# Second layer of a fused attention + MLP kernel: 128x128 matmuls among the scores, or 64x64 products with a written order for VectorE and ScalarE

## The chip, the cores and the metric

One core of one Trainium2 chip. The metric is the device time of one execution in microseconds (us), the median of the runs shown; lower is better.

## The reference

Attention with a root-mean-square norm of q and k over the head dimension, then a two-layer MLP with the tanh form of gelu. Eight batches, 12 heads, 448 positions, head dimension 64; `d_model` 768, `d_ff` 2048.

```python
q_n, k_n = rmsnorm(q, g_q), rmsnorm(k, g_k)            # x / sqrt(mean(x*x) + 1e-6) * g
scores = matmul(q_n, k_n.T) / sqrt(64)
attn = exp(scores - max(scores)); attn = attn / (sum(attn) + 1e-9)
x = matmul(attn, v).transpose(0, 2, 1, 3).reshape(8 * 448, 768)
h = x @ w_in                                            # 768 -> 2048
g = 0.5 * h * (1 + tanh(sqrt(2 / pi) * (h + 0.044715 * h**3)))
out = g @ w_out                                         # 2048 -> 768, float32
```

## The kernel before

The weights stay in SBUF in bf16 (`win`, `wout`). Batches go one after the other. Of each batch the 12 heads are three groups of four (index `c`), and the 448 keys are seven slices of 64 (index `t`): a *unit* (c, t) is four 64x64 matmuls of 448 columns, side by side in the array (two heads by two rows of the array), which give the scores of four heads for 64 keys, keys on the partitions. ScalarE turns a unit into exps (`ex`, L337; a constant `shift` takes the place of the maximum). VectorE adds the exps of a group over its slices (`key_sums`, L353 to L359), so that the sum over keys is one 64x64 step with a matrix of ones in place of seven; `products` (L384) makes the sums (`what` 0) or the values (`what` 1, seven steps of four matmuls). `turned`, `recip` and `spread` (L393, L399, L404) make the reciprocal of the sums and spread it over the partitions with VectorE's transposes; `quad_x` (L417) multiplies the values by it, into `xT`.

The first layer: 16 slices `f` of `d_ff`, six matmuls of 128x128 by 448 columns each. `mm1_pair` (L482) makes two slices in a PSUM tile of two banks with one gelu of 896 (L487); `mm1` (L431) one slice with one gelu of 448 (L437). From batch 2 on slices 0 to 3 go in pairs, 4 to 15 singly. The results go to `g`, which holds two batches, 896 rows, that is seven tiles of 128 rows.

The second layer (`mm2`, L452) takes a tile `i` of 128 rows and half of the 768 columns: 16 matmuls of 128x128 by 384 columns, summed over `f` in a bank of `ps_m`, copied to `osb` by VectorE (L462) or ScalarE (L460) and stored by SyncE. It lags: the second layer of a batch is laid among the scores of the next batch's attention.

The order is written by hand (`manual_schedule`): what Python records is what each engine's queue holds. `attention` (L511) lays out eight groups of units (`cuts`), and after each a number of second-layer matmuls (`shares`, `upto`): 96 in all in attention 2 (b = 1), 112 in each of attentions 3 to 8. So TensorE alternates between units or products, in the 64x64 form, and `mm2`, in the 128x128 form. `side` and `behind` hold what else is recorded at a group: loads two or three batches ahead, norms of the next batch, totals of squares. PSUM has eight banks: three tiles of two banks (`rounds`, taken in turn by `pair`) and two banks of `ps_m` in the steady part. GpSimd makes norms (L273), squares (L161) and the loads of v; `gpsimd_waits` makes it wait for a given tile by copying one element of it (`mark`, L673).

The first attention (`first_attention`) has another order and is not touched but for `unit` being cut in two, and for the place of one load of v. After the last first layer, 144 matmuls of the second layer remain; they end the kernel.

Of the kernel before, what the change touches and what calls it, by code (L numbers as in the profile page):

```python
# [17 lines left out]
def kernel(  # L18
# [19 lines left out]
    P = 128  # L38
# [23 lines left out]
    ps_m = ctx.enter_context(tc.tile_pool(name="ps_m", bufs=2, space=bass.MemoryType.PSUM))  # L62
    ps_t = ctx.enter_context(tc.tile_pool(name="ps_t", bufs=1, space=bass.MemoryType.PSUM))
    start = ctx.enter_context(ExitStack())
    ps_o = start.enter_context(tc.tile_pool(name="ps_o", bufs=1, space=bass.MemoryType.PSUM))
# [8 lines left out]
    def three():  # L74
        return len(rounds) == 3
# [164 lines left out]
    def rsqrt_last(b):  # L240
# [4 lines left out]
        if three():  # L245
            own, dst = pair("root")[:, 0], y
        else:
            own, dst = oall[0][:, S:], place(b, 1)
# [73 lines left out]
    exs, ess, oas = {}, {}, {}  # L322

    def unit(b, c, t):

        if (b, c) not in exs:
            exs[b, c] = exq.tile([P, NT, 2, S], BF16, tag="ex", name="ex")
        ex = exs[b, c]
        sc = pair("sc")
        for a in range(2):  # L330
            rs = slice(a * D, (a + 1) * D)
            for r in range(2):
                nc.tensor.matmul(  # L333
                    sc[r * R:(r + 1) * R, a, :S], kT[rs, c, t, r], qT[b][rs, c, :, r],
                    start=True, stop=True,
                )
        nc.scalar.activation(ex[:, t], sc[:, :, :S], AF.Exp, scale=scale, bias=shift)  # L337

    def added(b, c):

        return NT - 1 if b > 1 else (NT - 1, 0, NT - 2)[c] if b else 0

    def key_sums(b, c, t):

        n = added(b, c)
        if t > n or t == 0:
            return
        ex = exs[b, c]
        if t == 1:
            ess[b, c] = exq.tile([P, 2, S], BF16, tag="es", name="es")  # L350
        es = ess[b, c]
        if t == 1:
            nc.vector.tensor_add(es, ex[:, 0], ex[:, 1])  # L353
        elif t == n and n % 2 == 0 or c + 1 == NCH and t > 3:
            nc.vector.tensor_add(es, es, ex[:, t])  # L355
        elif t % 2:
            e2 = exq.tile([P, 2, S], BF16, tag="e2", name="e2")
            nc.vector.tensor_add(e2, ex[:, t - 1], ex[:, t])  # L358
            nc.vector.tensor_add(es, es, e2)  # L359
# [8 lines left out]
    def products(b, c, what, lo=0, hi=NT):  # L368

        if lo == 0 and three():  # L370
            o = oas["o", what] = pair("o")
            oas[what] = [o[:, r, :S] for r in range(2)]
        elif lo == 0:
            oas[what] = spare.pop() if spare else [o[:, :S] for o in oall]
        o = oas[what]
        es = [exs[b, c][:, t] for t in range(NT)]
        if not what and added(b, c):
            es[:added(b, c) + 1] = [ess[b, c]]
# [11 lines left out]
    def turned():  # L390
        st = oas["st"] = stp.tile([128, 2, S // 32, 32], F32, tag="st", name="st")
        for r in range(2):
            nc.vector.transpose(st[:, r].rearrange("p a b -> p (a b)"), oas[0][r])  # L393

    def recip():

        oas["rb"] = stp.tile([128, 2, S], F32, tag="rb", name="rb")
# [3 lines left out]
    def spread(rs=slice(0, 2)):  # L401
        m = S // 32
        rc = oas["rc"][:, rs.start * m:rs.stop * m]
# [9 lines left out]
    def quad_x(b, c):  # L413
        if c == 0:
            xT[b] = xp.tile([128, HP, S], BF16, tag="xT", name="xT")
        if three():
            nc.vector.tensor_mul(  # L417
                xT[b][:, 2 * c:2 * c + 2], oas["o", 1][:, :, :S], oas["rb"]
            )
            return  # L420
# [21 lines left out]
    osbs, by_act = {}, []  # L442

    def mm2(b, i, half, f, lo, hi):

        end = b + 1 == B and i + 1 == 2 * S // 128
        if f == 0:
            osbs["ps"] = ps_m.tile([128, 512], F32, tag="mm", name="o")
            if lo == 0:
                osbs[i] = op.tile([128, d_model], F32, tag="osb", name="osb")  # L450
        o, osb = osbs["ps"][:, :hi - lo], osbs[i]
        nc.tensor.matmul(  # L452
            o, g[:, f, i * 128:(i + 1) * 128], wout[:, f, lo:hi],
            start=(f == 0), stop=(f == nf - 1),
        )
        if f + 1 < nf:
            return
        last = end and hi == d_model
        if b + 1 == B and (lo == 0 or end) or by_act:
            nc.scalar.copy(osb[:, lo:hi], o)  # L460
        else:
            nc.vector.tensor_copy(osb[:, lo:hi], o)  # L462
        if half == 0 and not end:
            return
        for j in range(2):
            col = i * 128 + j * R
            r = ((b // 2) * 2 + col // S) * R
            cols = slice(lo if end else 0, hi)
            eng = nc.scalar if last and j else nc.sync
            eng.dma_start(  # L470
                out_v[col % S // R, r:r + R, cols], osb[j * R:(j + 1) * R, cols]
            )

    def mm1_pair(i, cs=range(HP), b=0, js=range(2)):

        if cs[0] == 0 and js[0] == 0:
# [9 lines left out]
        if cs[-1] == HP - 1 and js[-1] == 1:  # L486
            nc.scalar.activation(  # L487
                g[:, 2 * i:2 * i + 2, (b % 2) * S:(b % 2 + 1) * S], h[:, :, :S],
                AF.Gelu_apprx_tanh
            )  # L490

# [4 lines left out]
    def m2_parts(b):  # L496
        tiles = range(3) if b % 2 == 0 else range(3, 7)
        order = [(i, half) for i in tiles for half in range(2)]
        if b == 0:

            order.sort(key=lambda t: t[1])
        parts = [(i, half, half * HD, (half + 1) * HD) for i, half in order]
        if b + 1 == B:
            i, half, lo, hi = parts.pop()
            parts += [(i, half, lo, lo + HD // 2), (i, half, lo + HD // 2, hi)]
        return [
            lambda part=part, f=f: mm2(b, part[0], part[1], f, *part[2:])
            for part in parts for f in range(nf)
        ]

    def attention(b, m2, quota, side, behind, ends):  # L511


        units = [(c, t) for c in range(NCH) for t in range(NT)]
        cuts = (0, 3, 6, 9, 11, 13, 16, 18, 21)
        groups = [units[i:j] for i, j in zip(cuts, cuts[1:])]
        first, last, tail = (23, 16, 4) if b > 1 else (20, 14, 3)
        sums_at, x_at = {3: 0, 6: 1}, {4: 0}
        shares = (0, 13, 26, 35, 45, 58, 69) if b > 1 else (0, 13, 26, 34, 40, 53, 59)
        spread = quota - first - last - tail  # L520
        given = 0

        def upto(k):
            nonlocal given
            while given < k:
                m2.pop(0)()
                given += 1

        before = []
        for i, group in enumerate(groups):  # L530
            for fn in side.get(i, ()):
                fn()
            if b == 1 and i == 3:
                by_act.append(b)
            for c, t in group:
                unit(b, c, t)
            for c, t in before:
                key_sums(b, c, t)
            if i in x_at:
                products(b, x_at[i], 1)  # L540
                quad_x(b, x_at[i])
            elif i in sums_at:
                products(b, sums_at[i], 0)
                turned()
            if i == 0:
                n = first
            elif i < len(shares):
                n = spread * shares[i] // shares[-1] - spread * shares[i - 1] // shares[-1]
            else:
                n = last  # L550
            end = given + n

            upto(end - n // 2)
            if i in sums_at:
                recips()
            for c, t in group[:1 if i else 0]:
                key_sums(b, c, t)
            upto(end - n // 4)
            for c, t in group[1 if i else 0:-1]:
                key_sums(b, c, t)  # L560
            upto(end)
            before = group[-1:]
            for fn in behind.get(i, ()):
                fn()
        for fn in ends:
            fn()
        nc.scalar.preload_act_table_set(GELU_SET)

        if b == 1:
            for n in "qk":  # L570
                square(2, NCH - 1, n, nc.scalar)
        c = NCH - 1
        products(b, c - 1, 1)
        for c, t in before:
            key_sums(b, c, t)
        quad_x(b, c - 1)
        products(b, c, 0)
        turned()
        products(b, c, 1)
        recips()  # L580

        by_act.append(b)
        upto(quota)
        mm1_pair(0, early, b)
        quad_x(b, c)
        mm1_pair(1, early, b)
        by_act.clear()

    def first_attention(side, mid):

        for i in range(NCH * NT):
            for fn in side.get(i, ()):
                fn()
            unit(0, i // NT, i % NT)
            for fn in mid.get(i, ()):
# [139 lines left out]
    def turn_new(c, ts):  # L735
# [54 lines left out]
    m2 = []  # L790
    for b in range(B):
        m1, side, behind, ends = [], [], [], []
        if b == 0:
# [11 lines left out]
            side += [(1, lambda: late_loads(2, 0)), (3, lambda: gain(1, 2)),  # L805
                     (2, lambda: late_loads(2, 1), lambda: late_loads(2, 2))]
# [98 lines left out]
```

## Time and profile before

| | |
|---|---|
| three timed runs | 403.93, 404.03, 405.2 us; median 404.03 |
| span of the profiled execution | 402.9 us, from its first to its last instruction |
| granted TensorE clock | 1.000 |
| busy: TensorE, ScalarE, VectorE, GpSimd | 394.0, 280.8, 257.7, 123.6 us |
| first part, to the start of attention 2 | 50.9 us |
| attention 2 | 27.6 us, then its first layer to 96.6 |
| steady period (attentions 3 to 8, each with its first layer) | 46.95 us |
| what is left of the second layer | from 378.35 to the end |

The page gives the profiled execution's span and no other time of it; the timed runs have 1.1 us (median) more around it. In the rows PE is a matmul on TensorE, PEld a weight load, DVE VectorE, ACT ScalarE, POOL GpSimd, SP SyncE. A group of instructions reads: line, engine, operation, what it writes <- reads, shape, count | busy us, mean ns of one | idle us before it. Matmuls are pipelined: one is shown for some 0.33 us, while the next starts 0.16 or 0.19 us after it.

### The profile page before, as it was taken

To read this page: it belongs to the slowest core of one execution; us is meant where nothing else is said; L and a number is where in the kernel's file an instruction comes from. 1 tells how busy PE (TensorE), PEld (TensorE's weight loads), DVE (VectorE), ACT (ScalarE), POOL (GpSimd) and SP (SyncE) were. 2 spreads that over 40 slices of the span, in tenths; PEclk is the share of its full clock that TensorE was granted. 3 is DMA by queue.
4 is the path that set the end of the run, shared out by engine and by line. 5 is a ranking of instruction groups with operands and counts; after the bars stand their busy time and mean duration, and the time that the engine had idled before them with its cause. 6 is when DMAs were issued, how large, how long until landed. Compare 5 with 4: busy or idle time off the path is not lost.

```text
span 402.9 us, 8097 instructions
## 1 busy us (share of the span) xinstructions
PE 394.0 (98%) x3319; PEld 209.7 (52%) x3319; DVE 257.7 (64%) x436; ACT 280.8 (70%) x382; POOL 123.6 (31%) x104
## 2 busy tenths in 40 slices
PE   7799999999999999999999999999999999999996
PEld 3365555555555555554555555555555545555564
DVE  5999868975796369845699257963698405990010
ACT  6995498778974887857975789748878359744301
POOL 4993407454007230183004540072301800000000
PEclk9999999999999999999999999999999999999999
DMA  8999996998415964169612948149513511210033
GB/s 287 297 224 207 199 210 215 243 242 222 91 39 116 245 110 131 41 167 279 114 41 63 251 69 217 40 86 266 77 42 78 117 24 39 51 47 23 2 78 80
DMA packets 65577, 54.07 MB, mean 134 GB/s; under 512 B 37380, under 2 KB 60548, under 8 KB 65540
## 3 DMA queue, kind: packets, MB, share of 16 engines
q1 hardware_dynamic: 53184, 41.48, 38.7%
q0 software_dynamic: 12128, 11.80, 19.0%
q8 instruction: 26, 0.43, 0.4%
q10 hardware_dynamic: 228, 0.28, 0.2%
q14 instruction: 11, 0.09, 0.1%
HBM read 45.61 MB, written 11.01 MB: 141 GB/s over the span
## 4 chain that ended last, share of the span: by engine, by line
PE 92%; ACT 4%; DMA 2%; POOL 1%; SPq 0%; DVE 0%; issue 0%
PE o L452 38%; PE h L431 24%; PE t L482 12%; PE t L333 9%; PE t L384 8%; ACT ex L337 4%; DMA rawq<-in_q_dram 2%; POOL g L161 1%; PE tp L291 0%; PE o L384 0%; SPq L626 0%; PE os L384 0%; DVE ss L170 0%; ACT lg L195 0%; SPq L121 0%
## 5 line engine op out<-in xcount | busy, mean ns | idle before, releaser
L337 ACT ACTIVATE ex<-t,shift 128x896 bf16<-128x896 f32 x168 | 157.4, 1006 | 21.7 <-PE t L333 19.3
L452 PE MATMUL o<-wout,g 128*128 128x384 bf16 (+1 forms) x912 | 156.8, 324 | 0.0
L452 PEld LDWEIGHTS <-g 128*128 128x128 bf16 x912 | 83.6, 98 | 67.8 <-issue 18.8
L431 PE MATMUL h<-xT,win 128*128 128x448 bf16 x516 | 99.1, 352 | 0.0
L170 DVE TENSOR_REDUCE ss<-sq 128x14 f32<-128x896 f32 (+3 forms) x45 | 44.3, 999 | 48.9 <-ACT sq L159 45.9
L431 PEld LDWEIGHTS <-win 128*128 128x128 bf16 x516 | 50.5, 98 | 47.1
L437 ACT ACTIVATE g<-h 128x448 bf16<-128x448 f32 x86 | 46.6, 543 | 28.2 <-PE h L431 23.1
L462 DVE COPY osb<-o 128x384 f32<-128x384 f32 x41 | 22.7, 553 | 52.8 <-PE o L452 50.8
L333 PE MATMUL t<-qT,kT 64*64 64x448 bf16 x672 | 47.0, 359 | 2.6 <-ACT lg L195 1.0
L482 PE MATMUL t<-xT,win 128*128 128x448 bf16 x252 | 49.5, 353 | 0.0
L673 POOL COPY mark<-es 1x1 bf16<-1x1 bf16 x6 | 1.1, 176 | 131.8 <-DVE es L355 124.6
L487 ACT ACTIVATE g<-t 128x896 bf16<-128x896 f32 x21 | 18.4, 915 | 32.9 <-PE t L482 32.9
L273 POOL TENSOR_TENSOR nrmq<-rawq,rinv 128x896 bf16<-128x896 f32 (+1 forms) x21 | 34.8, 1658 | 10.0 <-DVE o L236 6.4
L482 PEld LDWEIGHTS <-win 128*128 128x128 bf16 x252 | 24.5, 98 | 22.6 <-issue 0.4
L273 POOL TENSOR_TENSOR nrmk<-rawk,rinv 128x896 bf16<-128x896 f32 x20 | 33.6, 1680 | 0.0
L333 PEld LDWEIGHTS <-kT 64*64 64x64 bf16 x672 | 17.4, 105 | 27.4 <-issue 20.3
L384 PE MATMUL t<-ex,vb 64*64 64x448 bf16 x588 | 31.6, 350 | 0.0
L460 ACT COPY osb<-o 128x384 f32<-128x384 f32 (+1 forms) x16 | 7.3, 458 | 31.4 <-PE o L452 31.4
L404 DVE STREAM_TRANSPOSE rb<-rc 128x896 f32<-128x896 f32 (+1 forms) x25 | 26.8, 1073 | 0.8
L384 PEld LDWEIGHTS <-vb 64*64 64x64 bf16 x672 | 20.2, 107 | 12.0 <-issue 3.0
L358 DVE TENSOR_TENSOR e<-ex 128x896 bf16<-128x896 bf16 x33 | 20.0, 606 | 9.7 <-ACT ex L337 9.4
L393 DVE STREAM_TRANSPOSE st<-t 128x448 f32<-128x448 f32 x42 | 24.6, 624 | 1.0 <-PE t L384 0.9
(93 smaller groups left out, 296.2 us busy)
## 6 DMA issues: line engine op xcount, KB each, us to landing
out_dram<-osb SPq DMA_DIRECT2D x54, 192.0 KB, 2.7
rawq<-in_q_dram SPq DMA_DIRECT2D x23, 448.0 KB, 4.6
rawk<-in_k_dram SPq DMA_DIRECT2D x23, 448.0 KB, 5.8
vb<-in_v_dram POOLq DMA_DIRECT2D x6, 672.0 KB, 6.5
win<-in_moe_w_in_dram POOLq DMA_DIRECT2D x8, 384.0 KB, 10.4
wout<-in_moe_w_out_dram POOLq DMA_DIRECT2D x2, 1536.0 KB, 22.3
vb<-in_v_dram POOLq DMA_DIRECT2D x2, 448.0 KB, 17.9
vb<-in_v_dram POOLq DMA_DIRECT2D x2, 224.0 KB, 12.1
```

The source lines that it names most:

```text
L170: nc.vector.reduce_sum(sss[b][:, seat(b, c), "qk".index(n), hs, ts], squares(b, c, n, hs, ts), axis=AX.X)
L273: eng.tensor_mul(nrms[n, b, c][:, ts].rearrange("p t a d -> p a t d"), raws[n, b, c][:, :, ts], root[:, :, ts].to_broadcast([P, 2, m, D]),)
L333: nc.tensor.matmul(sc[r * R:(r + 1) * R, a, :S], kT[rs, c, t, r], qT[b][rs, c, :, r], start=True, stop=True,)
L337: nc.scalar.activation(ex[:, t], sc[:, :, :S], AF.Exp, scale=scale, bias=shift)
L384: nc.tensor.matmul(o[r][a * D:(a + 1) * D], vb[b % 2][rs, 2 * c + a, i] if what else ones[rs], es[i][rs, a], start=(i == 0), stop=(i == n ...
L393: nc.vector.transpose(st[:, r].rearrange("p a b -> p (a b)"), oas[0][r])
L404: nc.vector.transpose(oas["rb"][:, rs].rearrange("p r s -> p (r s)"), rc.to_broadcast([128, (rs.stop - rs.start) * m, 32]),)
L431: nc.tensor.matmul(h[:, :S], win[:, c, f * 128:(f + 1) * 128], xT[b][:, c], start=(c == 0), stop=(c == HP - 1),)
L437: nc.scalar.activation(g[:, f, (b % 2) * S:(b % 2 + 1) * S], h[:, :S], AF.Gelu_apprx_tanh)
L452: nc.tensor.matmul(o, g[:, f, i * 128:(i + 1) * 128], wout[:, f, lo:hi], start=(f == 0), stop=(f == nf - 1),)
L462: nc.vector.tensor_copy(osb[:, lo:hi], o)
L482: nc.tensor.matmul(h[:, j, :S], win[:, c, f * 128:(f + 1) * 128], xT[b][:, c], start=(c == 0), stop=(c == HP - 1),)
```

## The change

Attentions 2 to 8 keep to the 64x64 form. `quartered` computes two parts (tile and half) in one PSUM tile of two banks: a step `r` is one `f` and four 64x64 matmuls of 384 columns. Each row of the array takes 64 of the 128 rows of `wout` and writes one bank; after 16 steps the rows change banks (`turn`), and 16 more steps add the other half of the sum. Before the change of banks `follows` makes TensorE's queue wait until the last matmul of the first turn has landed. Three such tiles, 96 steps, stand in an attention; in attentions 3 to 8 the 16 matmuls of 128x128 that remain (`whole`, half of tile 6) stand at the attention's end, before the first layer.

`attention` reads its order from strings: `r` a step, `u` a unit, `s` and `x` sums and values of the next group. A second string is VectorE's order: E copy of a finished tile of `quartered` out of PSUM, A and B adds of two pairs of slices at once (1792 elements), F and G the last adds (896), T, R, S `turned`, `recip`, `spread`, M `quad_x`; in attention 2 also L late loads, K the gain on kT that GpSimd waits for, a the totals of squares. A third entry gives the exps before which ScalarE makes a copy. Whatever heads VectorE's or ScalarE's list is recorded as soon as what it needs has been recorded. PSUM has four tiles of two banks in the steady part, and `ps_m` ends with the first attention. The third group adds six of its seven exps, so its sums take two steps. Slices 4 to 15 of the first layer go in pairs.

```diff
+    def add_exps(b, c, step):
+        ex = exs[b, c]
+        if step == "A":
+            es = ess[b, c] = exq.tile([P, 2, 2, S], BF16, tag="es", name="es")
+            nc.vector.tensor_add(es, ex[:, :2], ex[:, 2:4])
+        es = ess[b, c]
+        if step == "B":
+            nc.vector.tensor_add(es, es, ex[:, 4:6])
+        elif step == "F":
+            nc.vector.tensor_add(es[:, 0], es[:, 0], es[:, 1])
+        elif step == "G":
+            nc.vector.tensor_add(es[:, 0], es[:, 0], ex[:, 6])
...
+    def whole(i, o, lo, hi):
+        for f in range(nf):
+            nc.tensor.matmul(
+                o, g[:, f, i * 128:(i + 1) * 128], wout[:, f, lo:hi],
+                start=(f == 0), stop=(f == nf - 1),
+            )
+
+    def follows(mm):
+        tc.add_manual_dep(
+            nc.tensor.nop().ins, mm.ins.name,
+            mybir.DependencyInfo(mybir.DependencyClass.Sync, mybir.DependencyReason.DATA),
+        )
+
+    def quartered(parts, finished):
+        o = rounds.pop(0)
+        for turn in range(2):
+            for f in range(nf):
+                if turn and f == 0:
+                    follows(mm)
+                for r in range(2):
+                    bank = (r + turn) % 2
+                    (i, half), rs = parts[bank], slice(r * D, (r + 1) * D)
+                    for a in range(2):
+                        at = i * 128 + a * R
+                        mm = nc.tensor.matmul(
+                            o[a * R:(a + 1) * R, bank, :HD], g[rs, f, at:at + R],
+                            wout[rs, f, half * HD:(half + 1) * HD],
+                            start=(turn == 0 and f == 0), stop=(turn == 1 and f == nf - 1),
+                        )
+                if turn and f + 1 == nf:
+                    rounds.append(o)
+                    finished(o)
+                yield
...
+    STEADY = (
+        "2r u 2r u 12r uu 11r u 3r u 2r 3r u 4r u 4r u 5r uu 3r s 4r u 4r u 3r u 2r x 1r u 4r u 5r"
+        " uu 6r su 5r u 9r u 2r xsx",
+        "E0 A0 B0 F0 G0 T0 R0 A1 S0 B1 M0 F1 G1 T1 A2 R1 B2 F2 S1 T2 M1 R2 S2 M2",
+        {14: 1, 21: 2},
+    )
+    SECOND = (
+        "2r u 3r u 4r u 7r 1r u 7r u 3r u 5r uu 13r u 3r us 4r u 4r uu 7r u 1r xusu 2r u 7r u 1r u"
+        " 6r uu 7r x 6r s 3r x",
+        "A0 L0 B0 F0 G0 L1 T0 R0 K0 S0 a0 a1 M0 a2 T1 a3 R1 a4 S1 A2 a5 B2 F2 M1 T2 R2 S2 M2",
+        {7: 0, 14: 1, 21: 2},
+    )
...
-            lambda: w_out_part(0), lambda: load_v(1, 0, 2),
+            lambda: w_out_part(0),
             lambda: square(1, 2, "q", nc.gpsimd), lambda: square(1, 2, "k", nc.gpsimd),
-            lambda: w_out_part(1), lambda: load_v(1, 2, 4)),
+            lambda: w_out_part(1), lambda: load_v(1, 0, 2), lambda: load_v(1, 2, 4)),
...
-            elif f > 3:
-                mm1(b, f)
+            elif f + 1 == nf:
+                mm1_pair(f // 2, b=b, js=(0,))
+                mm1_pair(f // 2, b=b, js=(1,))
+            elif f % 2 and f > 3:
+                mm1_pair(f // 2, b=b)
```

More of the change, by code (lines that the diff above doesn't have):

```diff
@@ L368, in products @@
     def products(b, c, what, lo=0, hi=NT):
-        if lo == 0 and three():
-            o = oas["o", what] = pair("o")
-            oas[what] = [o[:, r, :S] for r in range(2)]
+        if lo == 0 and steady():
+            o = oas["o", c, what] = pair("o")
+            oas[what] = oas[c, what] = [o[:, r, :S] for r in range(2)]
         elif lo == 0:
@@ L441 @@
     out_v = out.rearrange("(r t) d -> t r d", t=NT)
[L442 to L465, printed above, removed]
+    osbs = {}
@@ L466, in mm2, with osb_of, store @@
+    def osb_of(i):
+        osbs[i] = op.tile([128, d_model], F32, tag="osb", name="osb")
+    def store(b, i, lo=0, hi=d_model, engs=(nc.sync, nc.sync)):
+        for j, eng in enumerate(engs):
             col = i * 128 + j * R
             r = ((b // 2) * 2 + col // S) * R
-            cols = slice(lo if end else 0, hi)
-            eng = nc.scalar if last and j else nc.sync
             eng.dma_start(
-                out_v[col % S // R, r:r + R, cols], osb[j * R:(j + 1) * R, cols]
+                out_v[col % S // R, r:r + R, lo:hi], osbs[i][j * R:(j + 1) * R, lo:hi]
@@ new lines, in evict @@
+    def evict(b, parts, o, eng):
+        copy = nc.scalar.copy if eng is nc.scalar else nc.vector.tensor_copy
+        for i, _ in parts:
+            if i not in osbs:
+                osb_of(i)
+        if parts[0][0] == parts[1][0]:
+            i = parts[0][0]
+            copy(osbs[i].rearrange("p (h d) -> p h d", h=2), o[:, :, :HD])
+            store(b, i)
+            del osbs[i]
+            return
+        for bank, (i, half) in enumerate(parts):
+            cols = slice(half * HD, (half + 1) * HD)
+            copy(osbs[i][:, cols], o[:, bank, :HD])
+            store(b, i, cols.start, cols.stop)
+            if half:
+                del osbs[i]
@@ L494 @@
     even, odd = early[::2], early[1::2]
[L496 to L509, printed above, removed]
@@ L511, in attention @@
-    def attention(b, m2, quota, side, behind, ends):
-        units = [(c, t) for c in range(NCH) for t in range(NT)]
[L515 to L548, printed above, removed]
-            else:
[L550 to L564, printed above, removed]
@@ L569, in attention, with final @@
         if b == 1:
[L570 to L583, printed above, removed]
+            for m in "qk":
+                square(2, NCH - 1, m, nc.scalar)
+        if b > 1:
+            half, i = b % 2, 6
+            o = pair("o")[:, 0, :HD]
+            whole(i, o, half * HD, (half + 1) * HD)
+            osb_of(i)
+            cols = slice(half * HD, (half + 1) * HD)
+            nc.scalar.copy(osbs[i][:, cols], o)
+            store(b - 1 - b % 2, i, cols.start, cols.stop)
+            del osbs[i]
         mm1_pair(0, early, b)
-        quad_x(b, c)
         mm1_pair(1, early, b)
-        by_act.clear()
+        made.add(("p", 1))
+        go_on()
+    def final(b):
+        last = 2 * S // 128 - 1
+        for i in range(last - 3, last + 1):
+            osb_of(i)
+            for half in range(2):
+                parts = [(half * HD, (half + 1) * HD)]
+                if half and i == last:
+                    parts = [(HD, HD + HD // 2), (HD + HD // 2, d_model)]
+                for lo, hi in parts:
+                    po = pair("o")[:, 0, :hi - lo]
+                    whole(i, po, lo, hi)
+                    if half == 0 or i == last:
+                        nc.scalar.copy(osbs[i][:, lo:hi], po)
+                    else:
+                        nc.vector.tensor_copy(osbs[i][:, lo:hi], po)
+                    if i == last:
+                        end = hi == d_model
+                        store(b, i, lo, hi, (nc.sync, nc.scalar if end else nc.sync))
+            if i < last:
+                store(b, i)
     def first_attention(side, mid):
@@ L788, in normed_both @@
             normed(b, c, n, eng)
-    m2 = []
     for b in range(B):
-        m1, side, behind, ends = [], [], [], []
+        m1, side, extra, ends = [], [], [], []
         if b == 0:
@@ L840 @@
                 m1.append((13, lambda n=n: square(b + 2, 2, n, nc.gpsimd)))
-                side.append((0, lambda n=n: total(b + 2, 2, n)))
+                extra.append(("first", lambda n=n: total(b + 2, 2, n)))
         if 0 < b and b + 1 < B:
-            side.append((0, lambda: gain(b + 1, 2)))
+            extra.append(("first", lambda: gain(b + 1, 2)))
         m1 = plan(*m1)
@@ L872 @@
                 tc.tile_pool(name="ps_x", bufs=1, space=bass.MemoryType.PSUM))
-            rounds.insert(0, ps_x.tile([128, 2, 512], F32, tag="t2", name="t2"))
-        attention(b + 1, m2, 96 if b == 0 else 112, plan(*side), plan(*behind), ends)
+            for i in (2, 3):
+                rounds.append(ps_x.tile([128, 2, 512], F32, tag=f"t{i}", name=f"t{i}"))
+            late_on.append(b)
+        attention(b + 1, plan(*side), plan(*extra), ends)
 _INS = ['q', 'k', 'v', 'g_q', 'g_k', 'moe_w_in', 'moe_w_out']
```

177 lines of the change are left out of this document (124 added, 53 removed).

## The prediction

> **What bounds the kernel now.** I read the page first (busy shares, the chain's shares by engine), then the chain of waits in order of time, then the groups of instructions inside one attention.
>
> ```profile
> span 402.9 us, 8097 instructions
> PE 394.0 (98%) x3319; PEld 209.7 (52%) x3319; DVE 257.7 (64%) x436; ACT 280.8 (70%) x382; POOL 123.6 (31%) x104
> ...
> PE 92%; ACT 4%; DMA 2%; POOL 1%; SPq 0%; DVE 0%; issue 0%
> ```
>
> TensorE is busy for 98% of the span and holds 92% of the chain; no other engine is over 70%. So time can only come out of TensorE's own sequence, and it is lost again wherever the new sequence makes TensorE wait. One steady period (attention of a batch, then its first layer) in the chain:
>
> ```profile
> 50.86 0.69 PE t L333 x12
> ...
> 284.45 0.69 PE t L333 x12
> 285.14 3.84 PE o L452 x23
> ...
> 291.90 0.69 PE t L333 x12
> 292.59 2.22 PE o L452 x13
> 294.81 0.50 PE t L333 x8
> ...
> 297.07 0.50 PE t L333 x8
> 297.57 1.32 PE t L384 x28
> ...
> 309.52 2.96 PE t L384 x60
> 312.48 0.76 PE o L452 x4
> 313.24 4.54 PE t L482 x24
> 317.78 13.62 PE h L431 x72
> 331.40 0.69 PE t L333 x12
> ```
>
> Columns are start, length, what, how many (attention 2 begins at 50.86). From 284.45 to 331.40 there is only PE: a period of 46.95 us, of which attention has 313.24 - 284.45 = 28.79 and the first layer 18.16. Three units of scores (12 matmuls) take 0.69 and two take 0.50, so one more unit, four matmuls side by side, is 0.19. Second-layer matmuls: (3.84 - 2.22) / (23 - 13) = 0.162 each. The group of three units is 0.69 - 3 x 0.19 = 0.12 longer than its units, the group of 13 matmuls 2.22 - 13 x 0.162 = 0.114 longer than its matmuls. So going from the 128x128 to the 64x64 form and back costs 0.12 + 0.114 = 0.234 us. From one 64x64 kind to another (297.07 to 297.57) it costs nothing: 0.50 + 1.32 is 2 + 7 steps of 0.189 and one 0.12 for the way in. The order written in `attention` goes out and back nine times; 112 x 0.162 + 45 steps x 0.189 (21 units, 21 of values, 3 of sums) + 9 x 0.234 = 28.75, against 28.79 in the trace, so the model holds.
>
> **What the change takes away.** In attentions 3 to 8 the 96 steps `r` of `quartered` run in the 64x64 form between units and products, and the 16 matmuls of `whole` stand at the end, next to the first layer, which is 128x128 anyway. Nine ways out and back become one: 8 x 0.234 = 1.87 us saved. The third group of heads now adds only six of its seven exps (`added` gives NT - 2), so its sums take two steps, not one: +0.19. TensorE's own work is then 96 x 0.162 + 16 x 0.162 + 46 x 0.189 + 0.234 = 27.07 against 28.79: 1.72 less. The first layer in pairs of `f` has the same 96 matmuls; its ScalarE work (two 448-wide pieces become one of 896) only shrinks.
>
> **What one step `r` costs.** Not in this trace: no 64x64 matmul has 384 columns.
>
> ```profile
> L452 PE MATMUL o<-wout,g 128*128 128x384 bf16 x112 | 19.8, 327 | 0.0
> L384 PE MATMUL t<-ex,vb 64*64 64x448 bf16 x84 | 4.5, 350 | 0.0
> L384 PEld LDWEIGHTS <-vb 64*64 64x64 bf16 x84 | 2.4, 107 | 1.5 <-issue 0.3
> ```
>
> Seven steps of the value products in 1.32 us are 0.189 for 448 columns, 0.422 ns per column; the 128x128 matmul's 0.162 for 384 columns is also 0.422 ns per column. Both stream at the same rate, so the lower bound for `r` is 0.162. The four weight loads of a step are busy 2.4 / 84 x 4 = 0.114 us together, under 0.162. The upper bound is the 0.189 of the only stream of this kind seen: four loads and four matmuls per step have not been shown to go out faster than that. I take 0.162, because load time and column rate both point to it.
>
> **The wait inside `quartered`.** Halfway, `follows` holds TensorE's queue until the last matmul of the first turn has landed; everything behind it (weight loads, units) is held. A matmul lands 0.327 after its start. In attentions 3 to 8 two steps of other kinds, 0.38 us, stand at each of the three turns ("uu", "uu", "su"), so the result is there when the queue arrives: cost 0, and without that cover 0.327 - 0.162 + about 0.1 for the restart = 0.27 each. In attention 2 the first turn ("7r 1r") has no cover: 0.27 once.
>
> **Where VectorE gives time back.** VectorE's order is now fixed: E0 A0 B0 F0 G0 T0 ... Its first work, E0 (copy of the first finished pair of parts), stands ahead of the adds although the exps that A0 needs are there earlier.
>
> ```profile
> 285.05 1.28 ACT L863 ACT_TABLE_LOAD   x1
> 286.34 1.01 ACT L337 ACTIVATE ex<-t,shift 128x896 bf16<-128x896 f32 x1
> ...
> L337 ACT ACTIVATE ex<-t,shift 128x896 bf16<-128x896 f32 x21 | 19.7, 1004 | 3.2 <-PE t L333 2.9
> L393 DVE STREAM_TRANSPOSE st<-t 128x448 f32<-128x448 f32 x6 | 3.5, 624 | 0.0
> L462 DVE COPY osb<-o 128x384 f32<-128x384 f32 x6 | 3.3, 553 | 2.3 <-PE o L452 2.3
> L359 DVE TENSOR_TENSOR es<-es,e 128x896 bf16<-128x896 bf16 x5 | 3.1, 624 | 0.2
> L404 DVE STREAM_TRANSPOSE rb<-rc 128x896 f32<-128x896 f32 x2 | 2.2, 1112 | 0.1
> L417 DVE TENSOR_TENSOR xT<-t,rb 128x896 bf16<-128x896 f32 x2 | 2.2, 1086 | 0.3 <-PE t L384 0.3
> L399 DVE RECIPROCAL rc<-st 128x28 f32<-128x28 f32 x3 | 1.0, 328 | 0.1
> ```
>
> Twice the width costs less than twice the time: transposes of 448 and 896 take 624 and 1112, a fixed part of 0.136. So an add of 1792 (A, B) is 2 x 0.624 - 0.136 = 1.11, at most 1.25; E0 is 2 x 0.553 - 0.136 = 0.97, at most the 1.09 of L417. Count from TensorE's first instruction of the attention, with 0.12 for the way in. The 32nd `r` starts after 31 x 0.162 + 6 units x 0.19 + 0.12 = 6.28, lands at 6.61, and E0 starts at 6.67 (0.06 for a semaphore, from the marks below). Then E0 0.97, A0 and B0 1.11 each, F0 and G0 0.62 each: G0 ends at 11.10. TensorE reaches the first sums "s" after 51 `r` and 11 units: 0.12 + 8.26 + 2.09 = 10.47. It waits 0.7 us, up to 0.9 with the hand-overs between dependent adds. ScalarE is not the cause: exp 0 starts 286.34 - 284.45 = 1.89 in, 19.7 / 21 = 0.94 each, so exp 6 (for G0) ends by 8.6. Until the second "s" VectorE has T0 1.17 (3.5 / 3), R0 0.33, A1, S0 1.11, B1, M0 1.09, F1, G1, in all 7.2, and TensorE 29 `r`, 7 units, sums and one value product, 7.5; with the 0.4 for the result that T0 awaits these are level. The same holds up to the third "s" (4.35 + 0.4 against 4.67). I take 0.85 for the three together. Net per attention 1.72 - 0.85 = 0.87, six times: 5.2 us.
>
> **Attention 2** has the same saving (1.87) less 0.27. Its VectorE order puts the totals a0, a1 of GpSimd's squares ahead of M0, and the gain K0, which GpSimd waits for, behind T0 and R0, which need the first "s".
>
> ```profile
> 60.18 0.45 DVE L320 TENSOR_SCALAR kT<-kT,gcols 128x896 bf16<-128x896 bf16 x1
> 60.69 0.18 POOL L673 COPY mark<-kT 1x1 bf16<-1x1 bf16 x1 [15.35 <-DVE kT L320]
> 61.59 1.68 POOL L161 TENSOR_TENSOR sq<-rawq 128x896 f32<-128x896 f32 x1 [0.72 <-DMA rawq<-in_q_dram]
> 63.23 1.68 POOL L161 TENSOR_TENSOR sq<-rawk 128x896 f32<-128x896 f32 x1
> ...
> 65.82 3.65 DVE L170 TENSOR_REDUCE ss<-sq 128x14 f32<-128x896 f32 x5
> ```
>
> K0 ends at 60.63 and the mark starts 0.06 later. From "s" on: result 0.4, T0 1.17, R0 0.33, K0 0.45, mark 0.25, squares 1.68 + 1.65, total a1 about 1.1, M0 1.09: 8.1 us. TensorE needs M0's PSUM tile for its third `quartered` after 16 `r`, 4 units, sums of seven steps, one value product and two more steps: 6.4. It waits about 1.7, plus 0.3 for `w_out_part(1)` (below). So attention 2 comes out at 1.6 - 2.0, some 0.4 longer. GpSimd's queue is then about 2 us late, which the next transposes have room for.
>
> **Queues that moved.** `load_v(1, 0, 2)` now goes out behind `w_out_part(1)` on GpSimd.
>
> ```profile
> L663 POOL DMA_DIRECT2D wout<-in_moe_w_out_dram x2: 1204/1213/1222, 26.8 to 32.0; - x2
> DMA to landing us min/median/max: 18.5/22.3/26.2
> ```
>
> The later half of `wout` landed by 32.0 + 26.2 = 58.2. Attention 2 now wants it at its 33rd `r`, 50.86 + 6.6 = 57.5, where before took it after 48 matmuls. Going out earlier and with 448 KB less ahead, it lands sooner by something between 0 and 2 us; I keep 0.3 of wait, between 0 and 0.7. The stores stay on SyncE; attention 2 stores halves, 12 in place of 6, the others 8 where 7 were the mean. Behind them in SyncE's queue stand loads for later batches and the transposes for the next one, which wait for GpSimd's products anyway: cost 0 as long as the copies are not late.
>
> **The sum.** -5.2 + 0.4 = -4.8. The profiled span is 402.9; the three timed runs have a median of 404.03, 1.1 more around it, which the change leaves alone. 404.03 - 4.8 = 399.2.
>
> **Rivals.** First, the orders fit and VectorE makes nobody wait. For it: VectorE is busy only 64%. Against: the row sums above. It gives 6 x 1.72 + 1.6 = 11.9 less: 392.1.
>
> Second, VectorE and ScalarE pace the attention at the upper ends of their costs: E0 1.09, A and B 1.25, hand-overs 0.2, which makes the waits 0.7 + 0.12 + 0.28 + 0.2 = 1.3 at the first "s" and 0.2 at each of the other two: 1.7 in place of 0.85. ScalarE, with two copies from PSUM moved into its queue ahead of the last exps, would do the same. Then 1.72 is cancelled, and with attention 2 the time is 404.4. The Trainium skill, TensorEngine Tiling (Array Packing), section PSUM Bottleneck, says that tiling speeds TensorE up but not the emptying of PSUM, which may become the bound; the trace of before, where copies wait for TensorE (2.3 us at L462), does not show that yet.
>
> Third, on the slower side: a step of four loads and four matmuls goes out no faster than the 0.189 seen. Then `r` costs 0.027 more: 96 x 0.027 = 2.6 per attention. The wait at the first "s" shrinks by (51 - 31) x 0.027 = 0.54, so a steady attention changes by -0.87 + 2.6 - 0.54 = +1.2 and the whole by 6 x 1.2 + 0.4 + 1.6 = 9.2: 413. It decides from a step of about 0.172 on, where 4.8 us are used up. For it: 49 instructions per us for 16 us on end, where before showed 42 for 3 us. Against: the equal time per column. The Trainium skill has a rule on this side: TensorEngine Tiling (Array Packing), section Restrictions, says column tiling turns the fast weight load off, and TensorE: Matmul & The Clock Gate, section LDWEIGHTS, gives columns / 1.2 GHz, so four loads of 64 in turn would be 213 ns, an estimate. The products' step of 189 ns, four such loads in it, disagrees.
>
> Fourth, the change does not do what it says: the 0.234 belongs to a change of operands, not of the array's form. Then some 17 ways out and back per attention cost 4.0 us where nine cost 2.1: 1.9 more instead of 1.87 less, 399.2 + 7 x 3.8, some 425. The border at 297.57 that costs nothing speaks against it.
>
> **How the numbers follow.** Forecast 0.50, first rival 0.14, second 0.12, third 0.20, fourth 0.04. Faster and slower are told apart from no change at 0.3%, 1.2 us. The forecast and the first rival are faster (0.64); of the second 0.10 lies within 0.3% and 0.02 beyond it; with the third and fourth, slower is 0.26. For 8 in 10 the range reaches down to the first rival, 392, and up to 409, into the third with steps of about 0.180.
>
> **What would show it.** In the chain after: attention of about 28 us in place of 28.79, its groups of L487 and L333 without 0.1 at each border; `r` at 0.162 (any 16 in 2.6). In the waits: TensorE's first matmul of the sums waiting for the add at L360, 0.7 to 0.9 in each of six attentions, and in attention 2 the third `quartered` waiting for L420 for some 1.7 us. Wrong if steps take over 0.17, if PE waits for ScalarE inside attentions, or if PE shows no wait for VectorE.

## The result: 400.12 us after, 4.5 us less

| | before | after |
|---|---|---|
| timed, four runs each | 404.62 us (403.93 to 405.48) | 400.12 us (399.46 to 400.39) |
| ratio after / before | | 0.9891, interval 0.987 to 0.9911 |
| span of the profiled execution | 402.9 us | 398.3 us |
| first part, to attention 2 | 50.86 | 50.89 |
| attention 2 and its first layer | 45.78 | 45.94 |
| six steady periods | 281.71 (46.95 each) | 276.65 (46.11 each) |
| rest of the second layer, to the end | 24.55 | 24.82 |

The change is faster by 4.5 us in the medians and by 4.6 us in the spans; 4.8 us were forecast. The profiled execution's own time is 400.39 us, 2.1 more than its span; it is the slowest of the four, 0.3 above their median. All of the gain is in the steady part, 281.71 - 276.65 = 5.06; the other three parts together give back 0.46, of which 0.27 lies behind TensorE's last matmul, in the last store.

From the page after, the busy times and the chain's shares:

```profile
PE 384.8 (97%) x5359; PEld 231.9 (58%) x5359; DVE 231.5 (58%) x358; ACT 281.6 (71%) x361; POOL 123.6 (31%) x104
PE 82%; DVE 7%; ACT 6%; DMA 2%; POOL 1%; issue 1%; SPq 0%; DVEq 0%
```

TensorE is busy for 9.2 us less, but its share of the chain fell from 92% to 82% and VectorE's rose from 0% to 7%: the chain now leaves TensorE. Where it does so is seen in the chain of waits of one steady period (start, length, what, how many):

```profile
142.92 0.45 PE t L487 x8
...
144.08 1.95 PE t L487 x48
146.03 0.38 PE t L333 x8
146.40 1.79 PE t L487 x44
...
149.44 0.96 DVE osb L505
150.39 1.01 DVE es L353
...
151.50 1.10 DVE es L356
...
152.62 0.64 DVE es L358
...
153.35 0.64 DVE es L360
...
154.03 0.38 PE t L385 x4
...
170.86 18.16 PE t L524 x96
189.02 0.45 PE t L487 x8
```

L487 is `quartered`, L524 the first layer (L461, `whole`, stands ahead of it), L505 the copy E, L353 to L360 the adds A, B, F, G, L385 sums and values. Twelve steps `r` take 1.95 (0.1625 each), eleven take 1.79, and the borders between L487 and L333 cost nothing (the first group, two steps in 0.45, has the 0.12 of the one way in). Then there are 4.6 us in which the chain is E0, A0, B0, F0, G0 on VectorE, and the first sums at 154.03 start when G0 has ended. The waits of TensorE (line waited for: us in all, times, longest) show the same wait in each of six attentions, and one in attention 2:

```profile
PE t L385 <- DVE es L360: 3.7, 6, 0.7
PE t L487 <- DVE xT L420: 1.2, 1, 1.2
```

Both waits that the prediction named are there, and no third one inside the steady attentions.

### The profile page after: what moved, and what is told of

Same layout as the page of the kernel before. It is cut to its first block, busy times and chain, and to the rows that moved or that the text cites. A ratio compares the mean times of both kernels' runs of the same rounds, so it can differ in the third digit from the quotient of the medians.

```text
span 398.3 us, 12138 instructions
## 1 busy us (share of the span) xinstructions
PE 384.8 (97%) x5359; PEld 231.9 (58%) x5359; DVE 231.5 (58%) x358; ACT 281.6 (71%) x361; POOL 123.6 (31%) x104
## 4 chain that ended last, share of the span: by engine, by line
PE 82%; DVE 7%; ACT 6%; DMA 2%; POOL 1%; issue 1%; SPq 0%; DVEq 0%
PE t L524 36%; PE t L487 22%; PE t L461 9%; PE t L385 9%; ACT ex L341 5%; PE t L333 5%; DVE es L356 2%; DMA rawq<-in_q_dram 2%; DVE es L353 2%; DVE osb L505 1%; DVE es L358 1%; DVE es L360 1%; POOL g L164 1%; PE h L434 1%; PE tp L294 0%
## 5 line engine op out<-in xcount | busy, mean ns | idle before, releaser
L524 PE MATMUL t<-xT,win 128*128 128x448 bf16 x756 | 144.8, 352 | 0.0
L487 PE MATMUL t<-wout,g 64*64 64x384 bf16 x2688 | 134.7, 323 | 1.4 <-DVE xT L420 1.2
L524 PEld LDWEIGHTS <-win 128*128 128x128 bf16 x756 | 73.8, 98 | 68.9 <-issue 0.7
L531 ACT ACTIVATE g<-t 128x896 bf16<-128x896 f32 (+1 forms) x70 | 58.1, 842 | 64.6 <-PE t L524 64.6
L487 PEld LDWEIGHTS <-g 64*64 64x64 bf16 x2688 | 79.4, 107 | 36.1 <-issue 4.1
L333 PE MATMUL t<-qT,kT 64*64 64x448 bf16 x672 | 57.7, 351 | 2.4 <-ACT lg L198 0.9
L461 PE MATMUL t<-wout,g 128*128 128x384 bf16 (+1 forms) x240 | 37.6, 316 | 0.0
L385 PE MATMUL t<-ex,vb 64*64 64x448 bf16 x588 | 31.4, 349 | 0.0
L461 PEld LDWEIGHTS <-g 128*128 128x128 bf16 x240 | 22.5, 98 | 15.0 <-issue 2.1
L333 PEld LDWEIGHTS <-kT 64*64 64x64 bf16 x672 | 21.8, 106 | 13.0 <-DVE kT L303 2.9
L385 PEld LDWEIGHTS <-vb 64*64 64x64 bf16 x672 | 20.9, 107 | 10.8 <-issue 0.8
L505 DVE COPY osb<-t 128x768 f32<-128x768 f32 x6 | 5.7, 957 | 35.9 <-PE t L487 23.2
L164 POOL TENSOR_TENSOR sq<-rawq 128x896 f32<-128x896 f32 (+1 forms) x9 | 13.6, 1511 | 36.8 <-DVE ss L173 32.7
L353 DVE TENSOR_TENSOR es<-ex 128x1792 bf16<-128x1792 bf16 x20 | 21.1, 1054 | 4.4 <-ACT ex L341 4.4
L420 DVE TENSOR_TENSOR xT<-t,rb 128x896 bf16<-128x896 f32 x21 | 22.6, 1076 | 0.9
```

The lines of the kernel that those rows point to most:

```text
L333: nc.tensor.matmul(sc[r * R:(r + 1) * R, a, :S], kT[rs, c, t, r], qT[b][rs, c, :, r], start=True, stop=True,)
L353: nc.vector.tensor_add(es, ex[:, :2], ex[:, 2:4])
L385: nc.tensor.matmul(o[r][a * D:(a + 1) * D], vb[b % 2][rs, 2 * c + a, i] if what else ones[rs], es[i][rs, a], start=(i == 0), stop=(i == n ...
L461: nc.tensor.matmul(o, g[:, f, i * 128:(i + 1) * 128], wout[:, f, lo:hi], start=(f == 0), stop=(f == nf - 1),)
L487: mm = nc.tensor.matmul(o[a * R:(a + 1) * R, bank, :HD], g[rs, f, at:at + R], wout[rs, f, half * HD:(half + 1) * HD], start=(turn == 0 and ...
L524: nc.tensor.matmul(h[:, j, :S], win[:, c, f * 128:(f + 1) * 128], xT[b][:, c], start=(c == 0), stop=(c == HP - 1),)
```

## The experiments

The periods below are the median of the six of a kernel, each from the start of a first layer (L524) to the start of the next: 46.95 before, 46.10 after. The start of attention 2 lay anywhere from 49.97 to 53.08 us in the profiles of these kernels, though no edit touches what lies ahead of it; so the periods, not the spans, are compared, and differences of medians of a few tenths are not read.

**E0 behind A0.** If the wait comes from the order of VectorE's list, it goes when the add whose exps are ready stands ahead of the copy that is not.

```diff
-        "E0 A0 B0 F0 G0 T0 R0 A1 S0 B1 M0 F1 G1 ...",
+        "A0 E0 B0 F0 G0 T0 R0 A1 S0 B1 M0 F1 G1 ...",
```

> Attentions 3 to 8: VectorE adds the first four exps (A0) before it copies the first finished tile (E0). Theory (VectorE's E0 at the head of its list gives back 0.78 us per steady attention): A0 fills the idle time before E0, G0 ends 0.9 to 1.0 us earlier, TensorE no longer waits at the first sums, period 46.10 to about 45.35, whole kernel about 4.5 us below the changed kernel (ratio to before about 0.978). Rival (the attention is paced by ScalarE or by VectorE's whole load, the wait only moves): TensorE waits as long somewhere later, within 1 us of the changed kernel (ratio about 0.989).

Measured: 395.28 us (395.04 to 397.89, six runs), ratio 0.9771 (0.9747 to 0.9795). VectorE in the same stretch of an attention (start, length, engine, line, what), first of the kernel after, whose attention starts at 142.92, then of this one, which starts at 144.39:

```profile
149.44 0.96 DVE L505 COPY osb<-t 128x768 f32<-128x768 f32 x1 [4.67 <-PE t L487]
150.31 1.08 DVE L353 TENSOR_TENSOR es<-ex 128x1792 bf16<-128x1792 bf16 x1
...
153.35 0.62 DVE L360 TENSOR_TENSOR es<-es,ex 128x896 bf16<-128x896 bf16 x1
```

```profile
150.02 1.09 DVE L353 TENSOR_TENSOR es<-ex 128x1792 bf16<-128x1792 bf16 x1 [3.79 <-ACT ex L341]
151.03 0.95 DVE L505 COPY osb<-t 128x768 f32<-128x768 f32 x1
...
153.74 0.63 DVE L360 TENSOR_TENSOR es<-es,ex 128x896 bf16<-128x896 bf16 x1
```

Counted from the attention's start, A0 begins at 7.39 after and at 5.63 here, and G0 begins at 10.43 after and at 9.35 here. In both VectorE stands idle before its first instruction, 4.67 and 3.79 us: after, it idles for the copy's tile while the exps lie ready. In the chain TensorE now runs through:

```profile
126.23 18.16 PE t L524 x96
144.39 0.45 PE t L487 x8
...
154.88 0.19 PE t L385 x4
...
171.53 13.62 PE t L524 x72
```

The period is 171.53 - 126.23 = 45.30 (median 45.31), 0.79 less, and the row of L385 waiting for L360 is gone. TensorE reaches the first sums at 154.88 - 144.39 = 10.49, where after starts them at 154.03 - 142.92 = 11.11: 0.62, the row's 3.7 / 6. The row counts from the end of the last matmul shown, but one matmul starts before the one ahead of it ends. So the wait's cost is seen better from the starts in the kernel after, where these are the three steps ahead of the first sums:

```profile
152.76 0.66 PE L487 MATMUL t<-wout,g 64*64 64x384 bf16 x12
```

Three steps are 0.49, so the sums were due at 153.25 and began at 154.03, 0.78 late: the whole of the 0.79. Six times 0.79 is 4.7, and the medians differ by 4.84. The wait at the first sums was the order alone, and the waits show no other in a steady attention.

**The 128x128 form.** The same order, waits, tiles and copies, but each of the 96 steps is one 128x128 matmul, 16 to a bank, with no wait in the middle. So the way between the forms is paid 21 times per attention, not once.

```diff
-                for r in range(2):
-                    bank = (r + turn) % 2
-                    (i, half), rs = parts[bank], slice(r * D, (r + 1) * D)
-                    for a in range(2):
-                        at = i * 128 + a * R
-                        mm = nc.tensor.matmul(o[a * R:(a + 1) * R, bank, :HD], ...)
+                nc.tensor.matmul(
+                    o[:, bank, :HD], g[:, f, i * 128:(i + 1) * 128],
+                    wout[:, f, half * HD:(half + 1) * HD],
+                    start=(f == 0), stop=(f == nf - 1),
+                )
```

> The changed kernel with one thing undone: the 96 steps of an attention are 128x128 matmuls of 384 columns again, 16 for each bank of the same PSUM tile, without the wait in the middle; lists, order, PSUM tiles and everything else as changed. Theory (the saving is the change of the array's form, 0.234 us per way out and back): 21 ways out and back in place of 1 per steady attention, +4.7 us, less the 0.78 us wait that vanishes, six times, and about +2.5 in attention 2: about 426 us, ratio 1.055. Rival (the saving comes from the four PSUM tiles, wider adds and written order, the form being worth little): about 400 us, ratio 0.99.

Measured: 425.71 us (424.99 to 426.38, four runs), ratio 1.0518 (1.0491 to 1.0545). Its chain:

```profile
131.74 18.16 PE t L518 x96
...
151.28 2.06 PE t L481 x12
...
156.64 0.31 PE t L333 x4
...
181.64 3.41 PE t L518 x18
```

L518 is its first layer and L481 its second. Twelve matmuls take 2.06, which is 12 x 0.1625 + 0.11, and a single unit 0.31, which is 0.19 + 0.12: both borders cost again what the prediction read from before. The period is 181.64 - 131.74 = 49.90. It has no wait for the sums, as the first experiment has none, so those two are compared: 49.90 - 45.31 = 4.59 for 20 more ways out and back, 0.23 each (the prediction had 0.234). What the change gains is the form, not the orders or tiles: with everything else as changed and the old form the kernel is slower than before by 5.2%, since its order was written for a form that pays for no border. The Trainium skill, TensorEngine Tiling (Array Packing), section Key Properties, says that a change of the tiling mode, not of the tile, drains TensorE. The runs agree as far as they go: the borders between the forms cost 0.23 us out and back, those between 64x64 products nothing; the drain itself is not seen in them.

**M0 ahead of the totals in attention 2.** The change's order puts a0 and a1 ahead of M0, for which TensorE waits.

```diff
-        "... R0 K0 S0 a0 a1 M0 a2 T1 a3 R1 a4 S1 ...",
+        "... R0 K0 S0 M0 a0 a1 a2 T1 a3 R1 a4 S1 ...",
```

> Attention 2: VectorE multiplies the first group's values (M0) before the totals a0 and a1, which wait for GpSimd. Theory (TensorE waits for M0's PSUM tile because two totals stand ahead of it): the 1.2 us wait of the third tile's first matmul goes, of which up to half comes back at the third sums, attention 2 from 27.7 to 26.5 to 27.1, whole kernel 0.6 to 1.2 us lower. Rival (GpSimd's late squares hold the attention anyway through the totals): no change within 0.3 us, the wait moves to the third sums.

Measured: 400.54 us (399.85 to 401.38, six runs), ratio 0.9899 (0.9879 to 0.992): no difference from the change. The waits of TensorE inside attention 2 of this kernel, and its chain there:

```profile
PE t L333 <- DVE st L395: 1.5, 1, 1.5
```

```profile
65.44 1.09 DVE xT L420
66.53 1.41 DVE ss L173 x2
...
69.55 0.66 DVE st L395
```

The wait for M0 (1.2 us) is gone, and a unit now waits 1.5 us for T1, which frees its PSUM tile and stands behind a0, a1 and a2. So the wait moved, as the rival said, but to T1 and not to the third sums. From its start to its first layer attention 2 took 27.98, against 27.67. With both edits at once:

> Both orders of VectorE changed: A0 before E0 in attentions 3 to 8, M0 before a0 and a1 in attention 2. Theory: the two add up, 5 to 6 us below the changed kernel, about 394.5 us, ratio 0.975 to 0.976. Rival (other engines pace the attentions): no lower than the better of the two alone.

Measured: 396.16 us (395.33 to 396.6, four runs), ratio 0.9786 (0.9761 to 0.981). The period is 45.31 again and the wait for T1 1.5 again; the interval overlaps that of the first edit alone. So the first edit brings its gain and the second none. Attention 2 of this profile has one wait more, for the later half of `wout`:

```profile
PE t L487 <- DMA wout<-in_moe_w_out_dram: 0.3, 1, 0.3
```

**A turn without cover.** On top of the first edit, the two units that stand at the first tile's change of banks are moved behind two steps of its second turn.

```diff
-        "2r u 2r u 12r uu 11r u 3r u ..."
+        "2r u 2r u 14r uu 9r u 3r u ..."
```

> On the order with A0 before E0: in attentions 3 to 8 the two units that stand at the first change of banks are moved two steps on, so that the wait for the last matmul of the first turn has nothing in front of it. Theory (the wait inside a finished tile costs nothing only because two steps of other kinds cover it; bare it costs 0.24, as in attention 2): +0.24 per steady attention, six times 1.4 us, period 45.31 to 45.55. Rival (TensorE's queue hides it, weight loads being pulled ahead): no change, period 45.31.

Measured: 397.54 us (396.57 to 397.8, six runs), ratio 0.9813 (0.9789 to 0.9838). In its chain the held queue shows as a break in the steps:

```profile
124.61 18.16 PE t L524 x96
...
143.92 1.98 PE t L487 x48
145.90 0.04 issue
145.94 0.52 PE t L487 x8
...
170.18 18.16 PE t L524 x96
```

Fourteen steps take 1.98 + 0.04 + 0.52 = 2.54 where 14 x 0.1625 is 2.275: 0.26. The period is 170.18 - 124.61 = 45.57, 0.26 more than without the edit; the prediction had 0.27 for a bare turn. Six times 0.26 is 1.6; the medians differ by 2.3, the ratios to before by 0.0042, which is 1.7 us. Attention 2, which the edit does not touch, took 0.65 more in this profile than in that of the first edit: there a unit waited 0.5 us for T1, in a chain that goes back over GpSimd's squares to a load of q. That scatter is of the size of the rest.

**E0 to ScalarE.** Another way to free VectorE's head: ScalarE makes the first copy too, ahead of its exp 7.

```diff
-        "E0 A0 B0 F0 G0 T0 ...", {14: 1, 21: 2},
+        "A0 B0 F0 G0 T0 ...", {7: 0, 14: 1, 21: 2},
```

> Attentions 3 to 8: the copy E0 goes from VectorE to ScalarE, ahead of the eighth exp; VectorE begins with A0. Theory (it was VectorE's place for E0 that cost 0.78 us, and ScalarE has about half a us to spare): TensorE's wait at the first sums goes as with A0 before E0, period 45.3 to 45.6. Rival (ScalarE paces the attention): the 0.7 us of the copy come back as waits of units for their tiles or of the last sums for the last exp, period 46.0 or more.

Measured: 399.38 us (399.24 to 400.29, six runs), ratio 0.987 (0.9848 to 0.9892). The period is 46.01, 0.09 less than after: of the 0.79 that the first edit gains, 0.70 comes back. Its waits of TensorE, and the chain at the place:

```profile
PE t L333 <- ACT osb L505: 2.1, 5, 0.4
```

```profile
144.30 6.42 ACT ex L341 x7
150.72 0.70 ACT osb L505
...
151.46 0.38 PE t L333 x4
```

The wait for G0 is gone and a wait for ScalarE has taken its place: units wait for the tile that ScalarE empties 0.7 us behind its seven exps. The Trainium skill, TensorEngine Tiling (Array Packing), section PSUM Bottleneck, advises both ScalarE and VectorE for emptying PSUM; here ScalarE makes two of the three copies of `quartered`'s tiles in a steady attention already, and the third there gained 0.09 where the right place on VectorE gained 0.79.

**T1 and S1 early in attention 2.** The first edit, and an order for attention 2 that has M0, T1, R1 and S1 ahead of most totals.

```diff
-        "... S0 a0 a1 M0 a2 T1 a3 R1 a4 S1 A2 a5 B2 F2 M1 ..."
+        "... S0 a0 M0 T1 a1 R1 S1 a2 A2 a3 B2 F2 a4 a5 M1 ..."
```

> A0 before E0 as above; in attention 2 VectorE takes M0 and the second group's transposes T1 ahead of all totals but a0, and the last totals behind the last adds. Theory (in attention 2 whichever of M0 and T1 stands behind GpSimd's squares holds a PSUM tile that TensorE needs; moving M0 alone handed the wait to T1): both waits go, some 0.2 to 0.5 us come back at the third sums, attention 2 from 27.7 to 26.5 to 27.0 us, 0.7 to 1.2 us below the order with A0 before E0 alone. Rival (ScalarE's pace or GpSimd's late squares set the length of attention 2): 27.5 us or more.

Measured: 394.65 us (394.58 to 395.87, five runs), ratio 0.9759 (0.9734 to 0.9783), the lowest median of all. The interval overlaps that of the first edit alone, and the profile does not credit attention 2: from its first start of L487 to that of attention 3 it took 46.15 us, against 45.94 in the kernel after and 45.93 with the first edit alone. So the 0.7 to 1.2 us that the theory promised are not seen. TensorE's waits inside attention 2, and the busy time of the engines from 68 to 81 us (the window, its length, then each engine's busy us and count):

```profile
PE t L487 <- issue: 0.6, 2, 0.4
PE t L524 <- DVE xT L420: 0.4, 1, 0.4
```

```profile
68.00:81.00 13.00, 12.79 (x234) 8.92 (x225) 12.57 (x18) 10.00 (x13) 6.09 (x7) 1.00 0.86 214
```

Neither M0 nor T1 is waited for now. VectorE is busy for 12.57 of the last 13 us (its columns come third, behind PE and PEld), and the first layer waits 0.4 us for M2. From 68.1 to the first layer's wait at 81.3 the chain stays on VectorE. In this stretch VectorE itself, with its totals of squares, has become the bound: an order can move its wait but takes no work out of it. The two short stalls that the view puts down to issue have no releaser in the profile; what they wait for stays open. The kernels with A0 first all beat the change and the kernel before; whether this one is better than the first edit alone is not resolved.

## Why the prediction was right, step by step

**The ways between the forms.** Read as 0.234 from groups of the chain before; 0.23 in the run with the old form. TensorE's own work in a steady attention was put at 27.07 us; without the wait it takes 171.53 - 144.39 = 27.14. So the first term, 1.72, was 46.95 - 45.31 = 1.64, and the measured price gives it again: eight ways at 0.23 less one step of 0.19 are 1.65.

**The step `r`.** Taken at the lower of two bounds, 0.162; measured 0.1625. It rested on equal time per column, and on loads that hide under the step. The groups after:

```profile
L487 PE MATMUL t<-wout,g 64*64 64x384 bf16 x2688 | 134.7, 323 | 1.4 <-DVE xT L420 1.2
L487 PEld LDWEIGHTS <-g 64*64 64x64 bf16 x2688 | 79.4, 107 | 36.1 <-issue 4.1
```

A load is shown for 107 ns, and 2688 of them fill only 79.4 us, 0.030 each: they overlap, four in 0.12 us, under the step. This refutes the third rival, which decided from steps of 0.172 on. The estimate beside it, 213 ns for four loads in turn, fails with it: the loads do not go in turn. The fourth rival fell with the old form's run: the price belongs to the form of the array, since the same operands cost 20 ways more in the other form.

**VectorE's list.** The place and mechanism were right: G0 was forecast to end 11.10 into the attention; it ends at 153.35 + 0.62 - 142.92 = 11.05, and the sums start at 11.11. That agreement is partly luck: E0 began at 6.52 and not at 6.67, and from there to the sums it took 4.59, where the five pieces had been added up to 4.43 without hand-overs. E0 was put at 0.97 and takes 0.96. The wait was put at 0.7 to 0.9 and costs 0.79, of which the waits' row shows 0.62. What was mis-sized is the part added for the second and third sums: of 0.85 in all, some 0.1 was laid there, and no wait is seen there. The two small errors, 1.64 for 1.72 and 0.79 for 0.85, almost cancel: 0.85 net in place of 0.87, 5.1 us over six periods in place of 5.2. The first rival's end, no wait, was not reached by the change, but in the steady attentions the first edit of the experiments reaches it with two names exchanged. The second rival did not happen: its waits at the second and third sums are absent and ScalarE holds nobody in a steady attention of the kernel after. Its remark on ScalarE holds with one copy more, as the sixth kernel showed.

**The turn.** Forecast 0 with cover, 0.27 without. In the chain after, the covered turn at 146.03 leaves eleven steps behind it at 1.79, 0 more. Bare, it costs 0.24 in attention 2 (405 ns between two steps in place of 162.5) and 0.26 in the fifth kernel.

**Attention 2.** Forecast 0.4 longer; from its start to its first layer it took 27.67, against 27.62, so 0.05. Two pieces of its chain, then five of TensorE's groups there by their starts:

```profile
56.18 1.91 ACT ex L341 x2
...
67.98 1.09 DVE xT L420
```

```profile
57.45 0.55 PE L333 MATMUL t<-qT,kT 64*64 64x448 bf16 x8
58.13 2.31 PE L487 MATMUL t<-wout,g 64*64 64x384 bf16 x52
...
61.11 0.39 PE L385 MATMUL t<-es,ones 64*64 64x448 bf16 x4
...
67.55 0.39 PE L333 MATMUL t<-qT,kT 64*64 64x448 bf16 x4
69.11 0.52 PE L487 MATMUL t<-wout,g 64*64 64x384 bf16 x8 [1.18 <-DVE xT L420]
```

The third tile of `quartered`, at 69.11, waits for M0 as forecast. Behind the unit at 67.55 (0.19) it was due at 67.74, so it is 1.37 late, not 1.7; 1.18 of that is shown as idle. From the first sums at 61.11 TensorE needed 6.63 to get there, where the prediction had 6.4, and VectorE and GpSimd had M0 ready after 69.07 - 61.11 = 7.96, where it had 8.1. The 0.3 before the 33rd step is there too: behind two units at 57.45 (0.38) it was due at 57.83 and starts at 58.13. But here the term was right by luck. The chain puts ScalarE's exps there (56.18 to 58.09), whose tile TensorE needs, and not the later half of `wout`, which went out at 31.3 and had landed by 31.3 + 25.8 = 57.1:

```profile
L754 POOL DMA_DIRECT2D wout<-in_moe_w_out_dram x2: 1209/1216/1222, 26.8 to 31.3; - x2
DMA to landing us min/median/max: 18.9/22.3/25.8
```

The margin is small: in the profile of the kernel with both edits the same step waits 0.3 for that half, which landed at 58.68. So 27.62 - 1.6 + 0.30 + 1.37 = 27.69, against 27.67: that the total was too long by 0.35 is the term for M0. In the profile of the kernel after TensorE waits for no DMA in attention 2, so the load of v that moved and the stores cost nothing there, as forecast.

**Around it.** The prediction's base, 404.03, was the median of three runs; with four it is 404.62. The 1.1 us around the span set one execution's span against the median of others; the four executions after have 2.1 us around their own spans. Forecast 4.8 less, measured 4.5; of the 0.9 between 399.2 and 400.12, 0.6 is the base. From the first part to the last store, four parts: 0.03 + 0.16 - 5.06 + 0.27 = -4.60.

## What to carry to other kernels

Price a change between array forms from the chain itself: groups of different length in the same form give the price of one step, and the remainder of a group that stands between two borders is the border; here 0.23 us out and back came out the same from the old kernel and from a run made to show it. When an engine's order is written by hand, look at what stands at the head of the list while the engine idles: an instruction whose operand comes last, ahead of one whose operands lie ready, costs the whole queue behind it, and exchanging the two was worth 4.8 us on top of the change's 4.5. Before work is moved to an engine that looks free on average, look at the stretch: ScalarE is busy for 71% of the span, and yet the 0.7 us of one copy between its seventh and eighth exps came back as waits of TensorE in full.

## What was not expected of the hardware

The rate of 64x64 products: four loads and four matmuls per 0.1625 us, 49 instructions per us in all 96 steps of an attention, with no loss against the 128x128 form (0.162 for 384 columns). And how few 64x64 steps hide a wait of TensorE on its own last matmul: with two of 0.19 us in between it costs nothing, with none 0.24 to 0.26 us.
